# Softmax attention mixed with linear attention: the order of the attention rounds turned from head group first to query block first

## The chip, the cores and the metric

The kernel runs on one core of one Trainium2 chip. The metric is the device time of one execution in microseconds (us), as the median of several runs. One execution of the kernel before was also profiled; durations below come from that one.

## The reference

```
x = A_x                                          # 2048 x 512, bf16
g = sigmoid((x * gate_w).sum(-1))                # one gate per row
a = softmax(q k^T / 4) v  @ A_wo                 # q,k,v = x @ A_wqkv, 32 heads of 16
phi(t) = where(t > 0, t + 1, exp(t)) + 1e-6
kv = phi(k)^T v ; z = sum over rows of phi(k)    # q,k,v = x @ B_wqkv, 32 heads of 16
b = (phi(q) kv) / (phi(q) z + 1e-6)  @ B_wo
out = g * a + (1 - g) * b                        # 2048 x 512
```

The scores of branch A are 32 heads x 2048 x 2048 exponentials. Branch B has no exponential over pairs, only those of phi.

## The kernel before

**Rounds.** Branch A is cut into 32 rounds. A round r has one query block `qc` (512 queries, four of them), one head group `t8` (8 heads, four of them) and a parity `par` (four heads j of the eight). In a round, all 16 key blocks `kb` of 128 keys are taken with the four heads: 64 units of 128 keys x 512 queries. `rinfo(r)` says which round is which. Before, the head group is the outermost: rounds 0 to 7 are head group 0 with all four query blocks, rounds 8 to 15 head group 1, and so on:

```python
def rinfo(r):
    t8, k = divmod(r, 8)
    return k // 2, t8, k % 2
```

**Who takes the exponentials.** Most units go to ScalarE: `emit_act_group` issues the score matmuls (K^T against `QP`, 32 rows each, packed by rows of the array) for a group of three units (PSUM banks 0, 1, 2) or two (banks 3, 4), in turn, and one exp over the group into a `PT` slot (L915). The last key blocks of a round may go to VectorE: `d_claim` gives it a whole key block (four units) at a time, `d_s1` reads scores from banks 5 and 6, one or two banks at a time, into `Lb` (L1158), and `chain_op` makes the exponential from bit operations on 128 x 2048 elements in four instructions (L1181, L1184, L1187, L1190). The results `Xb`, `Eb`, `Lb` and `PT` are multiplied with `V` (`emit_pv`, `emit_dpv`), packed by columns, and summed in bank 7. At a round's end `round_end` transposes bank 7 into `U` (L1005); after every second round `t_norm` normalises, multiplies with the gate and transposes into `OT` (L1017 to L1024).

**The other work** consists of tasks that share banks 5 and 6 with VectorE's scores: `t_xtr` (transposes of x), `t_kproj`, `t_qproj`, `t_v0`, `t_v1` (projections of branch A; `t_v0` makes V of head group 0 and `t_v1` V of the other three), `t_gate`, and for branch B `t_phik`, `t_z`, `t_g`, `t_kv`, `t_phiq`, `t_den`, `t_num`, and `t_out` (both output projections and the store). `t_qproj` writes a projection to `QT`, from which eight DMAs on SP's queue bring it masked into `QP` (three slots). `t_num` writes numerators to `OB`, and four transposing DMAs on the same queue bring them to `OBT`.

**What sets the order.** The program is put in order while it is built. A planner keeps a clock for each engine with a cost for each operation, and picks the next one for PE among candidates: a score group for ScalarE, scores for VectorE, value matmuls, tasks. Each task has a due time and an earliest start, both in rounds (`add(key, generator, due, nb, pre)`), and `progress()` is the round that ScalarE's groups have reached. `need(key)` finishes a task on the spot when a candidate can't do without it. Where PE would stand idle, the planner puts in filler matmuls on a tile `warm`. The engines then run their lists in order, with semaphores; nothing is reordered on the chip. All matmuls but those of `t_xtr` have the line L373, the DMAs L306 and L310.

**Buffers.** `OT` (normalised output of branch A) has four slots, one for each query block; its third slot holds the first weights `wA0` at the start. `OBT` (branch B) has four slots too, which lie on other tiles: two on `phiK`, one on `wBv`, one on `GT`. `D0` and `DR0` say from which progress and for which round VectorE may take key blocks.

Of the kernel before, what the change touches and what calls it, by code (L numbers as in the profile page):

```python
# [10 lines left out]
BF16 = mybir.dt.bfloat16  # L11
# [134 lines left out]
def bass_gated_mix__mha_block__linear_attn_block__prompt_kernel(  # L146
# [14 lines left out]
    NTB = S // 128  # L161
# [11 lines left out]
    with ExitStack() as es:  # L173
# [20 lines left out]
        phiK = SB("phiK", [128, NTB, D], BF16)  # L194
        U = SB("U", [128, 2, 512], FP32)
        Tn = SB("Tn", [128, 16, 32], BF16)
        OT = SB("OT", [128, 4, 4, 512], BF16)
        ebuf = SB("ebuf", [128, 2, 512], BF16)
        GT = SB("GT", [128, NCC, D], BF16)
        KVbd = SB("KVbd", [128, 4, 128], BF16)  # L200
# [25 lines left out]
        OB = wA[:, 1, :, :]  # L226
        outt = wA[:, 2, :, :]
        phk = phiK[:].rearrange("p t c -> p (t c)")
        OBT = [phk[:, 0:2048].rearrange("p (i n) -> p i n", i=4), phk[:, 2048:4096].rearrange("p (i n) -> p i n", i=4), wBv[:], GT[:]]
        woA = phk[:, 4096:6144].rearrange("p (i n) -> p i n", i=4)  # L230
        woB = phk[:, 6144:8192].rearrange("p (i n) -> p i n", i=4)

# [30 lines left out]
        r_phiK = [R(f"phiK{i}") for i in range(NTB)]  # L263
        r_U = [R("U0"), R("U1")]
        r_Tn = R("Tn")
        r_OT = [[R(f"OT{s}_{a}") for a in range(4)] for s in range(4)]
        r_e = [R("e0"), R("e1")]
        r_GT = [R(f"GT{c}") for c in range(NCC)]
        r_KVbd = R("KVbd")
# [5 lines left out]
        r_OBT = [[R(f"OBT{s}_{b}") for b in range(4)] for s in range(4)]  # L275
        r_const = R("const")
        r_ident = R("ident")
        r_mask = R("mask")
# [366 lines left out]
        def t_num(qc, q):  # L645
            s = qc % 2
            sl = q % 4
            b = yield "bank"
            rd = r_phiQT[s] + [r_KVbd]
            yield ("pe", rd, [r_bk[b]], 1.4)  # L650
            pe([mm(BK[b][:, 128 * i:128 * (i + 1)], phiQT[:, s, i, 128 * q:128 * (q + 1)], KVbd[:, i, :]) for i in range(4)],
               reads=rd, writes=[r_bk[b]], waves=1.4, cols=512)
            yield ("dve", [r_bk[b], r_denB], [r_OB[sl]])
            op(DV, lambda: nc.vector.tensor_tensor(OB[:, sl, :].rearrange("p (h d) -> p h d", h=32), BK[b].rearrange("p (h d) -> p h d", h=32),
                                                   denB[:, q, :].unsqueeze(2).to_broadcast([128, 32, 16]), ALU.mult),
               reads=[r_bk[b], r_denB], writes=[r_OB[sl], r_wA[1]], cost=0.69)
            yield "free"
            alias = (r_phiK[0:8], r_phiK[0:8], [r_wBv], r_GT)[qc]
            for i in range(4):
                raw = dma(OBT[qc][:, i, 128 * q:128 * (q + 1)], OB[:, sl, 128 * i:128 * (i + 1)], f"obt{sl}",  # L660
                          reads=[r_OB[sl]], writes=[r_OBT[qc][q]] + alias if i == 0 else [], transpose=True, lat=2.5 + i)
            for x in [r_OBT[qc][q]] + alias:
                x.w = _Raw(dma_sems[f"obt{sl}"][0], dma_sems[f"obt{sl}"][1], raw.t)
                x.r = {}

        def t_out(qc, q):
            so = qc
            sl = (4 * qc + q) % 4
            qb = 4 * qc + q
            b = yield "bank"  # L670
            ops_ = [(OBT[qc][:, i, 128 * q:128 * (q + 1)], woB[:, i, :], [r_OBT[qc][q]]) for i in range(4)]
# [168 lines left out]

        def kq_aps(r, kb, j):
            qc, t8, par = rinfo(r)
            s = (4 * t8 + qc) % 3
# [155 lines left out]

        def round_end(r):  # L1000
            qc, t8, par = rinfo(r)
            so = qc
            if r > par + 1:
                need(("pair", r - par - 1))
            op(DV, lambda: nc.vector.transpose(U[:, par, :], acc), reads=[r_acc], writes=[r_U[par]], cost=0.71)  # L1005
# [4 lines left out]
                tasks.insert(0, t)  # L1010

        def t_norm(qc, t8):
            so = qc
# [219 lines left out]
        GN = .9  # L1233
        XT = [("xtr", t) for t in range(NQC)]
        for t in range(NQC):
            add(("xtr", t), t_xtr(t), 0.25 * t - 0.3)
# [2 lines left out]
                add(("Q", 0, 0), t_qproj(0, 0), -0.19, pre=[("xtr", 0)])  # L1239
            add(("V0", t), t_v0(t), 0.25 * t - 0.15, pre=[("xtr", t)])  # L1240
        for tb in range(NTB):
            k = 15 - tb if tb > 11 else 4 + tb
            add(("V1", tb), t_v1(tb), V1D + V1S * k, V1N + V1S * k, pre=XT)
        add(("gate",), t_gate(), GD, GN, pre=XT)
        for t8 in range(1, 4):
            for k, t in enumerate((3, 0, 1, 2)):
                due = 8 * t8 - 1.2 + 0.25 * k
                add(("K", t8, t), t_kproj(t8, t), due, KN * t8 + 0.4 * k, pre=XT)
        for n in range(1, 16):
            t8, qc = divmod(n, 4)  # L1250
            add(("Q", qc, t8), t_qproj(qc, t8), 2 * n - 0.9, 2 * n - 1.5, pre=XT)
        for tb in range(NTB):
            add(("phiK", tb), t_phik(tb), 100 + tb, PKN + PKS * tb, pre=XT)
        PK = [("phiK", tb) for tb in range(NTB)]
        PK1 = PKN + PKS * 16
        add(("wq",), t_wq(), 116, PK1, pre=PK)
        add(("z",), t_z(), 117, PK1, pre=PK)
        for k, cc in enumerate((2, 3, 0, 1)):
            add(("G", cc), t_g(cc), 118 + k, PK1 + 0.2 + 0.8 * k, pre=PK + ([("G", 3)] if cc < 2 else [("G", 2)] if cc == 3 else []))
        GA = [("G", c) for c in range(4)]  # L1260
        G1 = PK1 + 3.6
        add(("wo",), t_wo(), 123, G1, pre=GA + [("z",)])
        add(("kv",), t_kv(), 124, G1, pre=GA)
        for qc in range(NQC):
            b0 = G1 + 0.6 + BS * qc
            for i in range(4):
                add(("phiQ", qc, i), t_phiq(qc, i), 130 + 20 * qc + i, b0 + BS / 6 * i,
                    pre=[("wq",)] + GA + [("num", qc - 2, q) for q in range(4) if qc >= 2])
            add(("den", qc), t_den(qc), 135 + 20 * qc, b0 + BS * 2 / 3,
                pre=[("phiQ", qc, i) for i in range(4)] + [("z",), ("gate",)] + [("num", qc - 1, q) for q in range(4) if qc])  # L1270
            for q in range(4):
                add(("num", qc, q), t_num(qc, q), 136 + 20 * qc + q, b0 + BS * 2 / 3 + 0.1 + 0.2 * q,
                    pre=[("den", qc), ("kv",), ("K", 3, 3), ("K", 3, 0), ("K", 3, 1), ("K", 3, 2), ("z",)])
# [145 lines left out]
```

The softmax here doesn't subtract the row's maximum and nothing guards it: scores larger than these inputs give would overflow.

## Time and profile before

| | |
|---|---|
| median of 6 runs | 777.78 us (777.18 to 778.91) |
| the profiled execution | 777.3 us; span of its instructions 775.5 us |
| granted TensorE clock in it | 0.999 |
| PE busy | 734.6 us (95%), fillers included |
| VectorE (DVE) busy | 701.9 us (91%) |
| ScalarE (ACT) busy | 758.7 us (98%) |
| exps on ScalarE | 655 groups: 327 of 1536 columns, 327 of 1024, one of 512 |
| key blocks on VectorE | 103 of 512 |

Busy times of one engine are unions: instructions that overlap are counted once. In a row of the groups, the numbers behind the bar are busy time in us and the mean of one in ns, and then the idle time of the engine ahead of them with what ended it. In a row of the timeline, the first two numbers are start and length in us, and `x` counts instructions that were merged into one row.

### The profile page before, as it was taken

Reading aid. Unit: us, or ns where it says so; the run is one execution under the profiler, and the core shown is the slowest. Engines: PE = TensorE matmul, PEld = TensorE weight load, DVE = VectorE, ACT = ScalarE, POOL = GpSimd, SP = SyncE. Lnnn points to the kernel's source line nnn. Section 1 sums busy time; section 2 is a strip of 40 time slices with the busy share of each in tenths; the row PEclk is TensorE's granted clock in tenths of the full one; section 3 lists DMA queues with packets and bytes.
Section 4 is the critical chain, followed back from the end, with each engine's and each line's share of the span. In section 5 each row is a group of like instructions: output and inputs, shape, how many; then the busy total and the mean of one; then the engine's idle time right before and its main releaser. Section 6 shows DMA issues by size and latency. Waiting matters only on the chain.

```text
span 775.5 us, 18041 instructions
## 1 busy us (share of the span) xinstructions
PE 734.6 (95%) x7845; PEld 221.3 (29%) x7905; DVE 701.9 (91%) x978; ACT 758.7 (98%) x692; POOL 10.8 (1%) x36
## 2 busy tenths in 40 slices
PE   8999999999999999999999999999999999999997
PEld 3322232322222222222222233222232232222222
DVE  4399999999999999988988999999899998998996
ACT  5999999999999999999999999999999999999995
POOL 4000000000000000010000000000000000000000
PEclk9999999999999999999999999999999999999999
DMA  7200000000000000102010000101001000011000
GB/s 175 89 3 2 8 2 7 3 1 8 2 8 2 4 6 1 36 1 59 4 56 8 2 8 4 23 11 22 14 8 21 11 1 28 15 22 35 9 21 28
DMA packets 31342, 14.93 MB, mean 19 GB/s; under 512 B 19104, under 2 KB 31264, under 8 KB 31264
## 3 DMA queue, kind: packets, MB, share of 16 engines
q1 hardware_dynamic: 29392, 13.00, 6.5%
q8 instruction: 62, 1.02, 0.5%
q10 hardware_dynamic: 1872, 0.79, 0.4%
q14 instruction: 16, 0.13, 0.1%
HBM read 6.55 MB, written 2.10 MB: 11 GB/s over the span
## 4 chain that ended last, share of the span: by engine, by line
ACT 88%; PE 5%; DVE 4%; issue 2%; DMA 1%; DVEq 0%; SPq 0%; ACTq 0%
ACT sb_PT L915 85%; PE ps L373 5%; ACT sb_ebuf L554 2%; DVE sb_Lb L1158 2%; DMA sb_xT<-in_A_x_dram 1%; DVE sb_Xb L1187 0%; DVE sb_Xb L1181 0%; DVE sb_Eb L1184 0%; DVE sb_phiK L558 0%; DVE sb_rowt L535 0%; SPq L306 0%; DVE sb_Lb L1190 0%; DVE sb_KT L476 0%; DVE sb_U L1005 0%; ACT sb_wA L683 0%
## 5 line engine op out<-in xcount | busy, mean ns | idle before, releaser
L915 ACT ACTIVATE sb_PT<-ps 128x1536 bf16<-128x1536 f32 (+1 forms) x655 | 751.2, 1432 | 6.3 <-PE ps L373 6.2
L373 PE MATMUL ps<-sb_QP,sb_KT 32*128 32x512 bf16 x2048 | 307.1, 384 | 22.7 <-ACT sb_PT L915 12.5
L1158 DVE TENSOR_SCALAR sb_Lb<-ps 128x1024 uint16<-128x1024 f32 (+1 forms) x272 | 261.1, 961 | 36.6 <-PE ps L373 33.4
L373 PE MATMUL ps<-sb_warm 128*17 128x512 bf16 (+9 forms) x2200 | 200.9, 342 | 1.3 <-POOL sb_warm L411 1.3
L373 PEld LDWEIGHTS ps<-sb_QP,sb_KT 32*128 32x128 bf16 x2048 | 78.3, 91 | 288.7 <-ACT sb_PT L915 222.2
L373 PE MATMUL ps<-sb_PT,sb_V 128*17 128x512 bf16 x1636 | 154.5, 384 | 1.1 <-DVE sb_U L1005 0.9
L1187 DVE TENSOR_TENSOR sb_Xb<-sb_Xb,sb_Lb 128x2048 bf16<-128x2048 bf16 x103 | 125.3, 1216 | 0.0
L373 PEld LDWEIGHTS ps<-sb_warm 128*17 128x17 bf16 (+2 forms) x2201 | 61.8, 90 | 53.1 <-issue 28.3
L1181 DVE TENSOR_SCALAR sb_Xb<-sb_Lb 128x2048 uint16<-128x2048 uint16 x103 | 70.8, 687 | 1.2
L1184 DVE TENSOR_SCALAR sb_Eb<-sb_Lb 128x2048 uint16<-128x2048 uint16 x103 | 70.5, 684 | 0.0
L1190 DVE TENSOR_SCALAR sb_Lb<-sb_Lb 128x2048 uint16<-128x2048 uint16 x103 | 70.4, 684 | 0.0
L373 PEld LDWEIGHTS ps<-sb_PT,sb_V 128*17 128x17 bf16 x1636 | 36.9, 87 | 94.5 <-issue 87.8
L373 PE MATMUL ps<-sb_Xb,sb_V 128*17 128x512 bf16 x412 | 40.1, 380 | 0.5 <-DVE sb_Xb L1187 0.4
L373 PE MATMUL ps<-sb_Eb,sb_V 128*17 128x512 bf16 x412 | 40.2, 381 | 0.3 <-DVE sb_Eb L1184 0.2
L373 PE MATMUL ps<-sb_Lb,sb_V 128*17 128x512 bf16 x412 | 40.2, 380 | 0.0
L373 PE MATMUL ps<-sb_xT,sb_wA 128*128 128x512 bf16 x91 | 27.3, 382 | 3.7 <-issue 2.4
L554 ACT ACTIVATE sb_ebuf<-ps 128x512 bf16<-128x512 f32 x32 | 26.2, 817 | 0.0
L1005 DVE STREAM_TRANSPOSE sb_U<-ps 128x512 f32<-128x512 f32 x32 | 22.7, 709 | 2.7 <-PE ps L373 2.5
L373 PE MATMUL ps<-sb_wA,sb_xT 128*128 128x128 bf16 (+1 forms) x128 | 19.5, 275 | 0.3 <-DVE sb_phiK L558 0.3
L373 PE MATMUL ps<-sb_phiK,sb_OT 128*128 128x512 bf16 x63 | 18.2, 382 | 0.2 <-issue 0.2
L373 PE MATMUL ps<-sb_xT,sb_wBx 128*128 128x512 bf16 x54 | 16.4, 382 | 1.5 <-issue 1.1
L476 DVE CAST sb_KT<-ps 128x512 bf16<-128x512 f32 x16 | 11.0, 685 | 7.4 <-PE ps L373 7.4
(87 smaller groups left out, 299.3 us busy)
## 6 DMA issues: line engine op xcount, KB each, us to landing
sb_QP<-sb_QT SPq DMA_DIRECT2D x120, 16.0 KB, 1.8
out_dram<-sb_wA SPq DMA_DIRECT2D x14, 128.0 KB, 1.7
sb_wA<-in_A_wqkv_dram SPq DMA_DIRECT2D x2, 512.0 KB, 6.9
sb_wBx<-in_B_wqkv_dram SPq DMA_DIRECT2D x2, 512.0 KB, 6.2
sb_xnat<-in_A_x_dram SPq DMA_DIRECT2D x2, 512.0 KB, 4.0
sb_xnat<-in_A_x_dram SPq DMA_DIRECT2D x3, 256.0 KB, 3.2
sb_wBv<-in_B_wqkv_dram SPq DMA_DIRECT2D x1, 512.0 KB, 9.4
sb_phiK<-in_A_wo_dram SPq DMA_DIRECT2D x1, 512.0 KB, 3.6
```

The costliest lines, as they stand in the source:

```text
L373: return lambda: nc.tensor.matmul(o, lhsT=l, rhs=r, start=start, stop=stop, skip_group_check=sg)
L476: op(DV, lambda: nc.vector.tensor_copy(KT[:, t8, 512 * t:512 * (t + 1)], BK[b]), reads=[r_bk[b]], writes=[r_KT[t8][t]], cost=0.69)
L554: op(AC, lambda: nc.scalar.activation(ebuf[:, s, :], BK[b], ACT.Exp), reads=[r_bk[b]], writes=[r_e[s]], cost=0.48)
L915: op(AC, lambda: nc.scalar.activation(PT[:, slot, 0:512 * n], ps[:, 512 * set_[0]:512 * (set_[0] + n)], ACT.Exp, scale=SCALE), reads=wr, w ...
L1005: op(DV, lambda: nc.vector.transpose(U[:, par, :], acc), reads=[r_acc], writes=[r_U[par]], cost=0.71)
L1158: op(DV, lambda: nc.vector.tensor_scalar(Lb[:, sl, 512 * k:512 * (k + n)], src, S1A, S1B, op0=ALU.mult, op1=ALU.add), reads=[r_bk[b] for b ...
L1181: op(DV, lambda: nc.vector.tensor_scalar(X, L, 0x7F, 0x3F00, op0=ALU.bitwise_and, op1=ALU.bitwise_or), reads=[rl], writes=[rx], cost=CH[0])
L1184: ev = op(DV, lambda: nc.vector.tensor_scalar(E_, L, 0xFF80, None, op0=ALU.bitwise_and), reads=[rl], writes=[re_], cost=CH[1])
L1187: ev = op(DV, lambda: nc.vector.tensor_tensor(xb, xb, lb, ALU.mult), reads=[rx, rl], writes=[rx], cost=CH[2])
L1190: ev = op(DV, lambda: nc.vector.tensor_scalar(L, L, float(EXP_SH), None, op0=ALU.add), reads=[rl], writes=[rl], cost=CH[3])
```

## The change

The rounds are ordered by query block first: rounds 0 to 7 are query block 0 with all four head groups. Q projections, their slots and K slots follow. With this order the normalised outputs of a query block are complete after eight rounds, so `OT` has three slots in place of four (`so = qc % 3`), `OBT` has two, both on `phiK`, and `t_num` of block qc waits for the outputs of block qc - 2. The output tasks of a block become due after its eighth round (`8 * qc + 8.1`), where they were due at round 26 and later. All K projections are due before round 6 (due times 1.3 to 2.1, 3.1 and 5.1) and the V projections around round 1.5 to 2.2, with their earliest starts at 0.3 for V and head group 1 of K. `D0` goes from 1 to 0.8, `DR0` from 0 to 1, `RES` from 0.2 to 0.5. `t_gate` and `t_z` are as they were.

```diff
@@
-        OT = SB("OT", [128, 4, 4, 512], BF16)
+        OT = SB("OT", [128, 3, 4, 512], BF16)
...
-        OBT = [phk[:, 0:2048].rearrange("p (i n) -> p i n", i=4), phk[:, 2048:4096].rearrange("p (i n) -> p i n", i=4), wBv[:], GT[:]]
+        OBT = phk[:, 0:4096].rearrange("p (s i n) -> p s i n", s=2, i=4)
...
         def t_qproj(qc, t8):
-            n = 4 * t8 + qc
+            n = 4 * qc + t8
...
         def t_out(qc, q):
-            so = qc
+            s = qc % 2
+            so = qc % 3
...
-                        yield ("wait", ("pair", 25 + 2 * qc))
+                        yield ("wait", ("pair", 8 * qc + 7))
...
-        D0 = 1
-        DR0 = 0
+        D0 = .8
+        DR0 = 1
...
         def rinfo(r):
-            t8, k = divmod(r, 8)
-            return k // 2, t8, k % 2
+            qc, k = divmod(r, 8)
+            return qc, k // 2, k % 2
...
-        RES = .2
+        RES = .5
...
-        V1D = 3
-        V1N = 1.5
-        V1S = .25
+        V1D = 1.3
+        V1N = .3
+        V1S = .06
+        K1D = 1.3
         MH2 = .9
-        KN = 6
-        PKN = 2.5
-        PKS = 0.65
-        BS = 2.4
-        GD = 1.6
-        GN = .9
+        GD = 1.9
+        GN = .5
...
-            k = 15 - tb if tb > 11 else 4 + tb
-            add(("V1", tb), t_v1(tb), V1D + V1S * k, V1N + V1S * k, pre=XT)
+            add(("V1", tb), t_v1(tb), V1D + (0.05 * (15 - tb) if tb > 12 else V1S * (tb + 4)), V1N, pre=XT)
...
-            for k, t in enumerate((3, 0, 1, 2)):
-                due = 8 * t8 - 1.2 + 0.25 * k
-                add(("K", t8, t), t_kproj(t8, t), due, KN * t8 + 0.4 * k, pre=XT)
-        for n in range(1, 16):
-            t8, qc = divmod(n, 4)
-            add(("Q", qc, t8), t_qproj(qc, t8), 2 * n - 0.9, 2 * n - 1.5, pre=XT)
+            for t in range(4):
+                if t8 == 1:
+                    due = K1D + (0.3, 0.55, 0.8, 0)[t]
+                    add(("K", t8, t), t_kproj(t8, t), due, V1N, pre=XT)
+                    continue
+                add(("K", t8, t), t_kproj(t8, t), 2 * t8 - 0.9 + 0.1 * t, 2 * t8 - 1.8 + 0.2 * t,
+                    pre=XT)
+        for q4 in range(1, 16):
+            qc, t8 = divmod(q4, 4)
+            due = K1D + 0.25 if q4 == 1 else 2 * q4 - 0.9
+            add(("Q", qc, t8), t_qproj(qc, t8), due, due - 0.6, pre=XT)
...
-                    pre=[("den", qc), ("kv",), ("K", 3, 3), ("K", 3, 0), ("K", 3, 1), ("K", 3, 2), ("z",)])
+                    pre=[("den", qc), ("kv",), ("K", 3, 3), ("z",)] + ([("out", qc - 2, q)] if qc >= 2 else []))
...
-                add(("out", qc, q), t_out(qc, q), 140 + 20 * qc + q, 26.05 + 2 * qc + 0.35 * q if qc < 3 else 31.9,
-                    pre=[("num", qc, q), ("wo",)] + [("V1", tb) for tb in range(NTB)] + ([("pair", 25 + 2 * qc)] if qc < 3 else []))
+                add(("out", qc, q), t_out(qc, q), 140 + 20 * qc + q, max(17.2 + 3.0 * qc + 3.0, 8 * qc + 8.1) + 0.3 * q if qc < 3 else 31.9,
+                    pre=[("num", qc, q), ("wo",)] + ([("pair", 8 * qc + 7)] if qc < 3 else []))
```

The earliest starts of branch B's tasks are near those before; written as numbers, they are 2.5 + 0.65 per `t_phik`, and 17.2 + 3.0 per query block for `t_phiq`, `t_den` and `t_num`, where the latter had 2.4 per block from 17.1.

More of the change, by code (lines that the diff above doesn't have):

```diff
@@ L265, in bass_gated_mix__mha_block__linear_attn_block__prompt_kernel @@
         r_Tn = R("Tn")
-        r_OT = [[R(f"OT{s}_{a}") for a in range(4)] for s in range(4)]
+        r_OT = [[R(f"OT{s}_{a}") for a in range(4)] for s in range(3)]
         r_e = [R("e0"), R("e1")]
@@ L274, in bass_gated_mix__mha_block__linear_attn_block__prompt_kernel @@
         r_outt = [R(f"outt{i}") for i in range(4)]
-        r_OBT = [[R(f"OBT{s}_{b}") for b in range(4)] for s in range(4)]
+        r_OBT = [[R(f"OBT{s}_{b}") for b in range(4)] for s in range(2)]
         r_const = R("const")
@@ L657, in t_num @@
             yield "free"
-            alias = (r_phiK[0:8], r_phiK[0:8], [r_wBv], r_GT)[qc]
             for i in range(4):
[L660 to L664, printed above, removed]
+                raw = dma(OBT[:, s, i, 128 * q:128 * (q + 1)], OB[:, sl, 128 * i:128 * (i + 1)], f"obt{sl}",
+                          reads=[r_OB[sl]], writes=[r_OBT[s][q]] + r_phiK[0:8] if i == 0 else [], transpose=True, lat=2.5 + i)
+            r_OBT[s][q].w = _Raw(dma_sems[f"obt{sl}"][0], dma_sems[f"obt{sl}"][1], raw.t)
+            r_OBT[s][q].r = {}
+            for x in r_phiK[0:8]:
+                x.w = r_OBT[s][q].w
         def t_out(qc, q):
-            so = qc
+            s = qc % 2
+            so = qc % 3
             sl = (4 * qc + q) % 4
@@ L670, in t_out @@
             b = yield "bank"
-            ops_ = [(OBT[qc][:, i, 128 * q:128 * (q + 1)], woB[:, i, :], [r_OBT[qc][q]]) for i in range(4)]
+            ops_ = [(OBT[:, s, i, 128 * q:128 * (q + 1)], woB[:, i, :], [r_OBT[s][q]]) for i in range(4)]
             ops_ += [(OT[:, so, a, 128 * q:128 * (q + 1)], woA[:, a, :], [r_OT[so][a]]) for a in range(4)]
@@ L842, in kq_aps @@
             qc, t8, par = rinfo(r)
-            s = (4 * t8 + qc) % 3
+            s = (4 * qc + t8) % 3
             return (KT[32 * j:32 * j + 32, t8, 128 * kb:128 * (kb + 1)], QP[32 * j:32 * j + 32, s, par, :],
@@ L1001, in round_end @@
             qc, t8, par = rinfo(r)
-            so = qc
+            so = qc % 3
             if r > par + 1:
@@ L1012, in t_norm @@
         def t_norm(qc, t8):
-            so = qc
+            so = qc % 3
             yield ("wait", ("gate",))
@@ L1252, in bass_gated_mix__mha_block__linear_attn_block__prompt_kernel @@
         for tb in range(NTB):
-            add(("phiK", tb), t_phik(tb), 100 + tb, PKN + PKS * tb, pre=XT)
+            add(("phiK", tb), t_phik(tb), 100 + tb, 2.5 + 0.65 * tb, pre=XT)
         PK = [("phiK", tb) for tb in range(NTB)]
-        PK1 = PKN + PKS * 16
-        add(("wq",), t_wq(), 116, PK1, pre=PK)
-        add(("z",), t_z(), 117, PK1, pre=PK)
+        add(("wq",), t_wq(), 116, 13, pre=PK)
+        add(("z",), t_z(), 117, 13, pre=PK)
         for k, cc in enumerate((2, 3, 0, 1)):
-            add(("G", cc), t_g(cc), 118 + k, PK1 + 0.2 + 0.8 * k, pre=PK + ([("G", 3)] if cc < 2 else [("G", 2)] if cc == 3 else []))
+            add(("G", cc), t_g(cc), 118 + k, 13.2 + 0.8 * k, pre=PK + ([("G", 3)] if cc < 2 else [("G", 2)] if cc == 3 else []))
@@ L1260, in bass_gated_mix__mha_block__linear_attn_block__prompt_kernel @@
         GA = [("G", c) for c in range(4)]
-        G1 = PK1 + 3.6
-        add(("wo",), t_wo(), 123, G1, pre=GA + [("z",)])
-        add(("kv",), t_kv(), 124, G1, pre=GA)
+        add(("wo",), t_wo(), 123, 16.6, pre=GA + [("z",)])
+        add(("kv",), t_kv(), 124, 16.6, pre=GA)
         for qc in range(NQC):
-            b0 = G1 + 0.6 + BS * qc
             for i in range(4):
-                add(("phiQ", qc, i), t_phiq(qc, i), 130 + 20 * qc + i, b0 + BS / 6 * i,
+                add(("phiQ", qc, i), t_phiq(qc, i), 130 + 20 * qc + i, 17.2 + 3.0 * qc + 0.5 * i,
@@ L1268, in bass_gated_mix__mha_block__linear_attn_block__prompt_kernel @@
                     pre=[("wq",)] + GA + [("num", qc - 2, q) for q in range(4) if qc >= 2])
-            add(("den", qc), t_den(qc), 135 + 20 * qc, b0 + BS * 2 / 3,
+            add(("den", qc), t_den(qc), 135 + 20 * qc, 17.2 + 3.0 * qc + 2.0,
                 pre=[("phiQ", qc, i) for i in range(4)] + [("z",), ("gate",)] + [("num", qc - 1, q) for q in range(4) if qc])
             for q in range(4):
-                add(("num", qc, q), t_num(qc, q), 136 + 20 * qc + q, b0 + BS * 2 / 3 + 0.1 + 0.2 * q,
-                    pre=[("den", qc), ("kv",), ("K", 3, 3), ("K", 3, 0), ("K", 3, 1), ("K", 3, 2), ("z",)])
+                add(("num", qc, q), t_num(qc, q), 136 + 20 * qc + q, 17.2 + 3.0 * qc + 2.1 + 0.2 * q,
+                    pre=[("den", qc), ("kv",), ("K", 3, 3), ("z",)] + ([("out", qc - 2, q)] if qc >= 2 else []))
```

## The prediction

> **What bounds the kernel now.** I read the page's busy times, slices and chain first, then the groups of instructions by shape, then two stretches of the timeline.
>
> ```profile
> span 775.5 us, 18041 instructions
> ...
> PE 734.6 (95%) x7845; PEld 221.3 (29%) x7905; DVE 701.9 (91%) x978; ACT 758.7 (98%) x692; POOL 10.8 (1%) x36
> ...
> DVE  4399999999999999988988999999899998998996
> ACT  5999999999999999999999999999999999999995
> ...
> ACT 88%; PE 5%; DVE 4%; issue 2%; DMA 1%; DVEq 0%; SPq 0%; ACTq 0%
> ```
>
> ScalarE is full from its first exp to its last and carries 88% of the chain. PE's 95% holds filler matmuls on `warm`; VectorE has idle time almost only in its first two slices (0 to 39 us).
>
> ```profile
> L915 ACT ACTIVATE sb_PT<-ps 128x1536 bf16<-128x1536 f32 x327 | 537.3, 1643 | 6.3 <-PE ps L373 6.2
> L915 ACT ACTIVATE sb_PT<-ps 128x1024 bf16<-128x1024 f32 x327 | 400.2, 1224 | 0.0
> L1158 DVE TENSOR_SCALAR sb_Lb<-ps 128x1024 uint16<-128x1024 f32 x140 | 170.7, 1219 | 13.9 <-PE ps L373 12.7
> L1187 DVE TENSOR_TENSOR sb_Xb<-sb_Xb,sb_Lb 128x2048 bf16<-128x2048 bf16 x103 | 125.3, 1216 | 0.0
> L1158 DVE TENSOR_SCALAR sb_Lb<-ps 128x512 uint16<-128x512 f32 x132 | 90.4, 687 | 22.6 <-PE ps L373 20.7
> ```
>
> The exps overlap: 537.3 + 400.2 is more than ScalarE's whole busy time. So an idle time of 6.3 us doesn't tell how long exps were late; their start times do.
>
> ```profile
> 89.58 0.80 ACT L554 ACTIVATE sb_ebuf<-ps 128x512 bf16<-128x512 f32 x1
> 90.05 2.58 ACT L915 ACTIVATE sb_PT<-ps 128x1536 bf16<-128x1536 f32 x2
> 92.29 0.84 ACT L554 ACTIVATE sb_ebuf<-ps 128x512 bf16<-128x512 f32 x1
> 92.77 24.30 ACT L915 ACTIVATE sb_PT<-ps 128x1536 bf16<-128x1536 f32 x21
> 116.79 0.77 ACT L554 ACTIVATE sb_ebuf<-ps 128x512 bf16<-128x512 f32 x1
> ```
>
> A pair of groups (1536 and 1024 columns) takes 92.29 - 90.05 = 2.24 us, a 512 one 0.48; start by start, the least distances are 1.331 and 0.904. The 21 groups from 92.77 then need 11 x 1.331 + 10 x 0.904 = 23.68, and took 24.02: 0.34 us of lateness that idle time doesn't show. Over the whole run: exps go from 9.77 to 766.17, 756.4 us. Their work is 327 x 1.331 + 327 x 0.904 + 33 x 0.478 + 0.16 (the gate's) = 746.8, and the last one's tail 0.28. So **9.3 us are hidden lateness**, spread evenly. The rest is head (9.8) and tail (775.5 - 766.17 = 9.3).
>
> ```profile
> 744.68 0.39 PE L373 MATMUL ps<-sb_QP,sb_KT 32*128 32x512 bf16 x4
> 745.01 0.60 PE L373 MATMUL ps<-sb_phiK,sb_OT 128*128 128x512 bf16 x2
> 745.55 0.39 PE L373 MATMUL ps<-sb_QP,sb_KT 32*128 32x512 bf16 x2
> 745.87 0.61 PE L373 MATMUL ps<-sb_PT,sb_V 128*17 128x512 bf16 x8
> 746.41 0.60 PE L373 MATMUL ps<-sb_phiK,sb_wBv 128*128 128x512 bf16 x2
> 746.95 0.39 PE L373 MATMUL ps<-sb_QP,sb_KT 32*128 32x512 bf16 x4
> ```
>
> From these starts I price PE: one step of 512 columns (a full matmul, up to four row-packed score matmuls, or four column-packed value matmuls) 0.215, and 0.10 more where the shape changes (0.33 for a score step, 0.54 for two full ones). A feed (the score matmuls of one exp group) may start when the group two before it has left its banks. With ends of 1.643 and 1.224 after their starts, 0.06 to the next matmul and its 0.39, PE can put about **1.46 us of work between two feeds** before the next exp is late; 0.48 more where an `ebuf` exp lies there.
>
> **The change part by part.** *What its name says.* Gate logits and sums of phi(K) are in both kernels the same 16 + 16 matmuls of 512 columns and five 32x32 transposes. Cost of that: nothing. What the diff does is to turn the rounds from head group first to query block first.
>
> *Exps moved off ScalarE.* In the changed kernel's instruction order VectorE takes 104 key blocks instead of 103. ScalarE loses one 1536 and one 512 group: -1.331 - 0.478 = **-1.81 us**, on the path.
>
> *VectorE pays for it:* one chain more (0.687 + 0.684 + 1.216 + 0.684 = 3.27) and 127 double plus 162 single reads of PSUM in place of 140 and 132: 30 x 0.687 - 13 x 1.219 = 4.76. Together +8.0 us on 701.9. Its 73.6 us of idle time covers it, so 0 here; uncovered it would be the whole 8.0.
>
> *Projections moved forward.* Counts are equal, places aren't. All 16 `t_v1` copies (549 ns) fall in rounds 0 to 2 (4, 6, 6 by the transposes that end rounds) instead of 1 to 5; the K projections of head groups 1, 2, 3 lie in rounds 0 to 5 instead of 6-7, 12-13, 18-19. Priced as above, PE's work without fillers in rounds 1 to 3 rises from 55.7 to 66.1 us, of about 69.5 us of ScalarE time; fillers fall from 10.2 to 2.9. That is where the cover shrinks. Interval by interval, work over 1.46 between feeds: before, 19 intervals, 1.75 us in all; after, 31 intervals, 3.89. The worst stands in round 2: one projection `K(1,2)`, put directly before the scores that read it because they need it at once, then a V projection forced in the same way (`V1(7)`), give 2.55 us of work between two feeds, 1.1 too much. Everything queued on PE behind waits, the next feed first, and ScalarE for that. So the direct count adds 3.89 - 1.75 = +2.1. But the 9.3 us measured are 5.3 times what is counted, for a late feed also follows from PE waiting for VectorE to empty a bank; in the same ratio the change would add 2.14 x 5.3 = +11.4. I take **+4.0**, nearer the direct count: the other waits were spread over the run and not tied to full intervals.
>
> [...]
>
> *The end of the run.* In the changed order two output stores follow the last QP transfers on SP; before, nine. What this saves in full intervals of rounds 26 to 31 is in the count. After the last exp the chain is the same (values, transpose, normalisation, transpose, output matmuls, copies, store), but four output matmuls follow the last transpose rather than nine. The four copies run one after the other either way (770.53 to 773.23), and can start one or two matmuls earlier: -0.2, between -0.4 and +1 if VectorE's last chain comes later than the last exp (it idled 1.36 us there).
>
> *Buffers and queues.* Three OT and two OBT slots make the numerators of block qc wait for the outputs of qc - 2; the order has these whole rounds earlier: 0. SP still issues 120 QP transfers and 64 transposes. QP parts now stand behind stores and transposes, but are planned 0.9 rounds (21 us) before their reader and land in 1.8: 0; if one were late, up to 1.8 us each.
>
> Sum: -1.81 - 0.2 + 4.0 = +2.0. The profiled execution took 777.3 (1.8 outside the span), so it becomes 779.3; the median of the runs is 0.5 above it at 777.78, so **779.8**.
>
> **The rivals.** *The crowd is absorbed (faster).* Lateness stays at 9.3 us: rounds 1 to 3 still hold less PE work than exp time, and overfull intervals may fall where ScalarE is behind anyhow. Then -2.0 remains: 775.8. It decides if added lateness stays under 0.4 us. Against it speaks the 2.55 us interval alone.
>
> *Lateness scales (much slower).* Between the transposes that end rounds 1 and 2 VectorE has 45 instructions of 27.6 us by their rows; each next one starts some 0.08 before the former ends, which leaves 24.0, beside 52 units of exp at 0.447 (a pair's 2.235 over five), 23.2. If banks 5 and 6 then stay held and feeds queue behind, +11.4 - 2.0 gives 787.2.
>
> *It doesn't do what it says, and the turn is neutral.* Gain and loss cancel with 2 us of added lateness: 777.8.
>
> **How the numbers follow.** A measurement of this kernel tells 0.2%, 1.56 us (776.2 to 779.3), from no change. The forecast's bounds are -2.0 + 2.1 = +0.1 and +9.4. Absorbed: 0.15, faster. Neutral: 0.12, same. Lateness in the full ratio: 0.05, slower. The forecast 0.68: 0.20 of it with under 3.6 us of added lateness, hence within 0.2%, and 0.48 above. That makes 0.15, 0.32 and 0.53. The range from 776.0 to 786.0 leaves out most of the absorbed case and the full ratio.
>
> **What would show it.** Right: 653 exp groups, a distance sum of 745.0, hidden lateness near 13 us with most of the growth before 100 us, and a gap of about 1 us around the K(1,2) projection near 75 us. Wrong: exps as even in rounds 1 to 3 as before (then 775.8), or lateness grown evenly through all rounds, which would point to VectorE and not to the crowd. A chain with VectorE above 10% would also contradict me.

## The result, and the profile after

The changed kernel takes **780.02 us** (median of 19 runs, 778.24 to 783.38) against 777.37 for the kernel before (median of 43 runs, 776.93 to 779.1): a ratio of 1.0032, 95% interval 1.0023 to 1.0040. The profiled execution took 780.02 with a span of 778.2, so 1.8 us lie outside the span as before. In eight of the 14 profiles here, whichever kernel, the first exp starts near 11.4 us instead of 9.7 (run 2 below shows why); spans of single profiles are therefore compared by their parts. The ratio and its interval are those on record; here and below, a ratio need not be the quotient of the two medians.

The page of the changed kernel (lines of the source stand one higher than before: the exps are L916, VectorE's reads of scores L1159):

```profile
span 778.2 us, 17861 instructions
...
PE 730.8 (94%) x7750; PEld 220.1 (28%) x7817; DVE 706.7 (91%) x999; ACT 757.9 (97%) x690; POOL 10.3 (1%) x36
...
DVE  4499899899999998999899999989999999999995
...
ACT 83%; PE 8%; DVE 6%; issue 2%; DMA 1%; DVEq 0%; SPq 0%; ACTq 0%
```

And the groups of instructions, shapes kept apart:

```profile
L916 ACT ACTIVATE sb_PT<-ps 128x1536 bf16<-128x1536 f32 x326 | 529.1, 1623 | 9.2 <-PE ps L373 9.1
L916 ACT ACTIVATE sb_PT<-ps 128x1024 bf16<-128x1024 f32 x327 | 393.1, 1203 | 0.3 <-PE ps L373 0.3
...
L1159 DVE TENSOR_SCALAR sb_Lb<-ps 128x1024 uint16<-128x1024 f32 x127 | 154.7, 1218 | 10.2 <-PE ps L373 9.0
L1188 DVE TENSOR_TENSOR sb_Xb<-sb_Xb,sb_Lb 128x2048 bf16<-128x2048 bf16 x104 | 126.5, 1217 | 0.0
L1159 DVE TENSOR_SCALAR sb_Lb<-ps 128x512 uint16<-128x512 f32 x162 | 110.7, 686 | 23.7 <-PE ps L373 22.5
```

One group of 1536 columns less, the single 512 one gone, 104 key blocks on VectorE. ScalarE's share of the chain fell from 88% to 83%, PE's rose from 5% to 8%. Exps go from 9.86 to 769.25. By the prediction's distances their work is 326 x 1.331 + 327 x 0.904 + 32 x 0.478 + 0.16 = 744.97, the last one's tail 0.19, so 14.2 us are lateness, where before it was 9.33:

| us | before | after | difference |
|---|---|---|---|
| work of the exps | 746.78 | 744.97 | -1.81 |
| lateness, start to 100 us | 1.61 | 3.89 | +2.28 |
| lateness, 300 to 325 and 450 to 475 us | 0.23 | 3.62 | +3.39 |
| lateness elsewhere | 7.49 | 6.72 | -0.77 |
| head, the last exp's own tail, and what follows it | 19.37 | 19.02 | -0.35 |
| span | 775.5 | 778.2 | +2.7 |

The lateness of each stretch is the sum of the distances between exp starts, less the least distance of each shape. Two stretches have grown, and the second is one that the prediction had not named. This is the first, in the timeline (start, length, then what ran):

```profile
75.75 0.39 PE L373 MATMUL ps<-sb_QP,sb_KT 32*128 32x512 bf16 x3
...
76.07 1.04 PE L373 MATMUL ps<-sb_xT,sb_wA 128*128 128x512 bf16 x4
76.15 0.71 DVE L535 STREAM_TRANSPOSE sb_rowt<-ps 128x512 f32<-128x512 f32 x1
76.89 0.17 DVE L536 COPY sb_gl<-sb_rowt 128x16 f32<-128x16 f32 x1
...
77.10 0.26 ACT L539 ACTIVATE sb_eg<-sb_gl 128x64 f32<-128x64 f32 x1 [0.66 <-DVE sb_gl L536]
...
77.26 1.43 ACT L916 ACTIVATE sb_PT<-ps 128x1536 bf16<-128x1536 f32 x1
...
77.53 0.82 PE L373 MATMUL ps<-sb_wA,sb_xT 128*128 128x384 bf16 x4
...
78.61 0.60 PE L373 MATMUL ps<-sb_QP,sb_KT 32*128 32x512 bf16 x5
...
79.04 1.02 ACT L916 ACTIVATE sb_PT<-ps 128x1024 bf16<-128x1024 f32 x1 [0.35 <-PE ps L373]
```

The four matmuls at 76.07 are `K(1,2)`, those at 77.53 `V1(7)`, as predicted; the scores at 78.61 come behind them and the exp at 79.04 is 0.45 us late. But the larger wait, 0.77 us, is ahead of that. The exp of the gate (L539) stands in ScalarE's list and waits for VectorE's last transpose of the gate logits (L535, L536), and the score exp at 77.26 is queued behind it, though its scores were there.

The second stretch shows in a table of windows (start and end, length, then the busy time and number of instructions of PE, weight load, VectorE, ScalarE and GpSimd; the first number behind these is the granted TensorE clock):

```profile
299.70:303.10 3.40, 2.44 (x24) 0.64 (x20) 3.01 (x5) 3.40 (x5) 0.00 (x0) 1.00 0.00 0
303.10:306.50 3.40, 3.40 (x29) 0.70 (x33) 2.58 (x5) 2.84 (x3) 0.00 (x0) 0.50 0.02 5
463.60:467.00 3.40, 2.34 (x24) 0.71 (x27) 3.07 (x5) 3.40 (x5) 0.00 (x0) 0.99 0.08 19
467.00:470.40 3.40, 3.40 (x33) 0.66 (x25) 2.57 (x4) 2.56 (x3) 0.00 (x0) 0.50 0.00 0
```

From 303.1 and from 467.0 us, PE runs at **half its clock**; in the trace's record of the clock both stretches last 3.413 us. The stretch ahead of each is thin: 24 matmuls, 2.44 and 2.34 us busy of 3.40. Both are ends of rounds: VectorE transposes bank 7 in them (at 301.59 and 465.43 us), and the planner put only single filler matmuls there. Over the rest of the run fillers are not fewer than before: behind round 3 the records have 1820 column fillers on `warm`, against 1748. It is their places that have changed. At half clock a score step takes 0.56 to 0.60 us instead of 0.39, the next feeds come late, and ScalarE idles (2.84 and 2.56 us busy of 3.40). The mean clock is 0.997 to 0.998 in the seven shortest runs that have a clock on record (778.24 to 778.65), 0.995 in the profiled one, and 0.991 to 0.992 in the three longest (782.49 to 783.38). A half-clock window takes 0.0022 of the mean (half of 3.413 us in 778), and the half clock at the very end takes 0.0004 in the profiled run and up to 0.0017 in others (run 5). By that estimate the runs have one, two or three windows. In the 80 runs of the kernel before beside the experiments the mean clock was 0.999 to 1.0, but for four at 0.997.

### The profile page after: what moved, and what is told of

Read it like the earlier page. It is cut to its first block, busy times and chain, and to the rows that moved or that the text cites. A ratio compares the mean times of both kernels' runs of the same rounds, so it can differ in the third digit from the quotient of the medians.

```text
span 778.2 us, 17861 instructions
## 1 busy us (share of the span) xinstructions
PE 730.8 (94%) x7750; PEld 220.1 (28%) x7817; DVE 706.7 (91%) x999; ACT 757.9 (97%) x690; POOL 10.3 (1%) x36
## 4 chain that ended last, share of the span: by engine, by line
ACT 83%; PE 8%; DVE 6%; issue 2%; DMA 1%; DVEq 0%; SPq 0%; ACTq 0%
ACT sb_PT L916 81%; PE ps L373 8%; ACT sb_ebuf L554 2%; DVE sb_Lb L1159 2%; DVE sb_Xb L1188 1%; DMA sb_xT<-in_A_x_dram 1%; DVE sb_Xb L1182 0%; DVE sb_Eb L1185 0%; DVE sb_U L1006 0%; DVE sb_rowt L535 0%; DVE sb_Lb L1191 0%; DVE sb_V L525 0%; DVE sb_Tn L1021 0%; DVE sb_xnat L558 0%; DVE sb_OT L1025 0%
## 5 line engine op out<-in xcount | busy, mean ns | idle before, releaser
L916 ACT ACTIVATE sb_PT<-ps 128x1536 bf16<-128x1536 f32 (+1 forms) x653 | 749.4, 1413 | 9.6 <-PE ps L373 9.4
L1159 DVE TENSOR_SCALAR sb_Lb<-ps 128x512 uint16<-128x512 f32 (+1 forms) x289 | 265.4, 920 | 33.9 <-PE ps L373 31.5
L373 PE MATMUL ps<-sb_warm 128*17 128x512 bf16 (+8 forms) x2101 | 192.9, 341 | 1.5 <-POOL sb_warm L411 1.3
L373 PEld LDWEIGHTS ps<-sb_warm 128*17 128x17 bf16 (+2 forms) x2105 | 59.8, 91 | 49.4 <-issue 27.2
L373 PE MATMUL ps<-sb_phiK 128*128 128x512 bf16 x54 | 16.6, 382 | 1.7 <-issue 1.1
```

The lines of the kernel that those rows point to most:

```text
L373: return lambda: nc.tensor.matmul(o, lhsT=l, rhs=r, start=start, stop=stop, skip_group_check=sg)
L916: op(AC, lambda: nc.scalar.activation(PT[:, slot, 0:512 * n], ps[:, 512 * set_[0]:512 * (set_[0] + n)], ACT.Exp, scale=SCALE), reads=wr, w ...
L1159: op(DV, lambda: nc.vector.tensor_scalar(Lb[:, sl, 512 * k:512 * (k + n)], src, S1A, S1B, op0=ALU.mult, op1=ALU.add), reads=[r_bk[b] for b ...
```

## Experiments

Two explanations are weighed. The crowd: the projections that were moved into rounds 0 to 2 make PE and VectorE late. The clock: thin stretches of PE's work bring half-clock windows, which make the feeds late.

**1. The thin places filled.** The changed kernel with nine filler steps put into PE's finished list, eight of them as below and one near 303 us behind a transpose of bank 7: the planner and every other engine's order are untouched.

```diff
+        zf = [mm(acc[32 * j:32 * j + VW, :], warm[:, 0:VW], warm, start=False, stop=False, sg=True) for j in range(4)]
+        more = [(pvat[k], n, []) for k, n in {153: 2, 242: 3, 281: 3}.items()]
...
+            PE.ops[at:at] = [(w if k == 0 else [], f, False, None) for k, f in enumerate(zf * n)]
```

> The changed kernel, order and semaphores untouched, with nine more column-packed filler steps of 512 columns on the zero tile, put where PE stands idle in the trace of after: two near 300.2 us, one near 302.5, three near 464.2, three near 537.5. Clock theory (the two stretches of 3.41 us at half clock in the profile of after, from 303.1 and 467.0 us, cost by themselves some 1.7 us each, and come because too few columns stream in the 3.41 us before): no half-clock stretch is left in most runs, the lateness of the exps falls from 14.1 to about 10.7 us, the median falls by 2.5 to 3.5 us to 776.5 to 777.5. Crowd theory (late exps around 303 and 468 us come from PE work and VectorE waits in the order, the low clock only follows from an idle PE): the order is the same, so time stays within 1 us of 780.0, or grows by up to 2 us for the added steps.

Measured: 778.81 us (12 runs), ratio 1.0015, interval 1.0004 to 1.0026. Both windows are gone and lateness in their slices fell from 3.62 to 0.87 us, but one stands at 513.0 us now, and its slice has 1.84 us (0.57 in run 9, where it is gone). So the clock is a cause, and nine steps don't fill every thin place: the mean clocks are 0.995 to 0.997 in all runs but one. The time and the lateness that the clock theory expected (776.5 to 777.5, and 10.7 us; the profile has 13.1) were therefore missed.

**2. The kernel before, filled.** Two filler steps of the same kind near 510 us, its thinnest place.

> The kernel before, order and semaphores untouched, with two more filler steps near 510.4 and 511.4 us. Clock theory: its runs fall into two heaps, about 777.2 and 778.9, because one place (508 to 512 us) is thin enough to lower the clock in about half of the runs; with the steps the upper heap goes, nearly all runs are 777.0 to 777.5, and the median moves by 0 to -0.3. Crowd theory: the two heaps stay as they are.

Measured: 777.23 us, ratio 0.9998, interval 0.9988 to 1.0007. Nothing to gain there: the kernel before hardly has half-clock windows. The two heaps stay, eight runs at 776.9 to 777.4 and four at 778.9 to 779.0, so the thin place doesn't make them. The profiled run (779.01) is one of the upper heap, and its first exp starts at 11.50 us instead of 9.77. The eight matmuls of the first projections, ahead of that exp, tell why. First the profile of the kernel before, then this run's:

```profile
6.60 1.89 PE L373 MATMUL ps<-sb_xT,sb_OT 128*128 128x512 bf16 x8 [0.83 <-DMA sb_xT<-in_A_x_dram]
```

```profile
6.49 3.57 PE L373 MATMUL ps<-sb_xT,sb_OT 128*128 128x512 bf16 x8 [0.71 <-DVE sb_xT L464]
```

From start to start one takes 0.427 us here and 0.215 there: PE still runs at half clock. The trace's record of the clock begins with the first full clock, at 10.77 us here and at 6.46 there, and the mean of 1.0 leaves out what lies ahead of it. All 14 profiles divide that way: with full clock by 6.46 us the first exp is at 9.64 to 9.99 (six), with full clock from 10.06 us or later at 11.34 to 11.55 (eight). So the 1.7 us between the heaps are a matter of the clock after all, at the start of the run.

**3. The gate earlier.** `GD` from 1.9 to 1.2 in the changed kernel, so that its exp isn't queued in the crowd near 75 us.

> The changed kernel with the gate's due time at 1.2 rounds in place of 1.9, so that its four matmul groups, transposes and its exp are over before the K(1,2) and V projections of round 2 (the planner then orders all of the run anew; 104 key blocks on VectorE as before). Crowd theory: lateness between 60 and 95 us falls from about 2.4 us to under 1, and the time falls by as much or more. Clock theory says the same of these 35 us (0.8 us there was the gate's exp waiting for VectorE), and that the rest of the run depends on how many thin places the new order has: 1.7 us more or less for each.

Measured: 779.45 us, ratio 1.0024, interval 1.0014 to 1.0034. Lateness before 100 us is 4.12 instead of 3.89: it has only moved to 70 us, where a K projection waits for the copy of a V projection (L525) that stands behind a normalisation on VectorE, and the feed behind both is 1.56 us late. Two windows of half clock (539.5 and 730.7 us) are there too. So moving the gate's exp alone doesn't cure the crowd; as all of the order changed with it, the run doesn't price it.

**4. Fillers made thin in the kernel before.** The converse of the first: the same kernel and order, but the planner's column fillers stream 64 columns instead of up to 512.

```diff
-pe([mm(acc[32 * j:32 * j + VW, 0:w], warm[:, 0:VW], warm[:, 0:w], start=False, ...) for j in range(4)],
+pe([mm(acc[32 * j:32 * j + VW, 0:64], warm[:, 0:VW], warm[:, 0:64], start=False, ...) for j in range(4)],
```

> The kernel before with the same order, but each of its column-packed filler steps streams 64 columns in place of 128 to 512: less PE work, nothing else changed. Clock theory: counted from the trace of before without these columns, some 15 windows of 3.41 us fall under 0.47 of streaming; each lowers the clock for one window and costs 1 to 1.7 us, so +12 to +25 us (789 to 802), and the granted clock falls to about 0.96. Crowd theory: PE has less to do and the exps bound the time, so 777.4 or up to 2 us less, at any clock.

Measured: 798.49 us, ratio 1.0271, interval 1.0251 to 1.0291. Less work for PE, and 21 us more. From the page, and from a table of windows around 577 us:

```profile
PEclk9977999999999999999989999999969999999899
```

```profile
574.00:577.20 3.20, 2.36 (x40) 0.87 (x37) 2.69 (x6) 3.20 (x5) 0.00 (x0) 1.00 0.02 5
577.20:590.80 13.60, 13.47 (x134) 4.18 (x126) 10.63 (x14) 10.88 (x10) 0.00 (x0) 0.50 0.00 1
```

The clock record has 21 windows of 3.413 us at half clock (four in a row from 577.2), and lateness rose from 9.33 to 28.91 us: 0.93 per window. The mean clock is 0.954 in this profile, where it is 0.999 in that of the kernel before. This settles that matmuls which compute nothing held the clock here, and gives a mean price of a window.

**5. All thin places filled, with waits.** 32 filler steps in the changed kernel instead of nine (26 in the expectation).

> The changed kernel with its order untouched and 26 filler steps of 512 columns (9 from the run before, 17 more) in the thin places that are left: near 164, 231 to 234, 279 to 281, 511 to 513, 538, 727 to 729, 745 and 748 us. If half-clock windows are what the first 100 us don't explain, none are left: granted clock 0.999, lateness of 100 to 750 us as in the kernel before, span 775.4 to 775.8 with the early head, time 777.2 to 777.6. So the change would be level with the kernel before: -1.81 (ScalarE's units) and -0.35 (tail) against +2.3 (lateness before 100 us). Rival: the turned order has lateness of its own in the later rounds, which fillers don't cure: 778.5 to 780 at a clock of 0.999, or the fillers delay the feeds and cost more.

Measured: 793.94 us, ratio 1.0199, interval 1.0184 to 1.0215. The rival's second half came true. The timeline tells why:

```profile
165.12 0.39 PE L373 MATMUL ps<-sb_PT,sb_V 128*17 128x512 bf16 x4
166.39 0.70 DVE L1011 STREAM_TRANSPOSE sb_U<-ps 128x512 f32<-128x512 f32 x1
167.15 0.53 PE L373 MATMUL ps<-sb_warm 128*17 128x512 bf16 x4 [1.64 <-DVE sb_U L1011]
167.60 0.61 PE L373 MATMUL ps<-sb_QP,sb_KT 32*128 32x512 bf16 x3
...
168.26 2.37 ACT L918 ACTIVATE sb_PT<-ps 128x1536 bf16<-128x1536 f32 x2 [1.54 <-PE ps L373]
```

These fillers write bank 7, so at a round's end they wait for its transpose, here for 1.64 us, in a list that is run in order; the feed behind them waits as well, and the clock of PE, now truly idle, falls to half on top (four windows, mean clock 0.990).

**6. The 104th key block by itself.** The kernel of the fifth run with `d_claim` stopped at 103 key blocks; only the last round's order differs.

```diff
-            if r >= NR or progress() < D0:
+            if r >= NR or progress() < D0 or sum(claimed) >= 103:
```

> The kernel with 26 filler steps, with VectorE's key blocks stopped at 103 instead of 104: order equal up to the last round, where four units go back to ScalarE. Prices the prediction's unit term by itself. If the 1.81 us lie on the path: +1.8 against the run beside it (779.0 to 779.4). Rival: the 104th key block is worth less, since the last round ends with VectorE's chains and values, which come earlier without it: +0.5 or less.

Measured: 793.24 us; the two kernels' windows of half clock vary too much for the medians to tell. Their two profiles, with the same four windows and the same head, have spans of 791.2 and 793.2. The last run below does it cleanly.

**7. The crowd alone, without the turn.** The kernel before with the V and K projections moved forward as in the change.

```diff
-            k = 15 - tb if tb > 11 else 4 + tb
-            add(("V1", tb), t_v1(tb), V1D + V1S * k, V1N + V1S * k, pre=XT)
+            add(("V1", tb), t_v1(tb), 1.3 + (0.05 * (15 - tb) if tb > 12 else .06 * (tb + 4)), .3, pre=XT)
...
+                if t8 == 1:
+                    due, nb = 1.3 + (0.3, 0.55, 0.8, 0)[t], .3
+                else:
+                    due, nb = 2 * t8 - 0.9 + 0.1 * t, 2 * t8 - 1.8 + 0.2 * t
```

> The kernel before with its rounds not turned, but with the V projections of t_v1 due and allowed as in the changed kernel (due 1.3 to 2.2, start 0.3), and the K projections of head group 1 too (1.3 to 2.1), those of groups 2 and 3 in rounds 2 to 5: the crowd alone, 103 key blocks. If the crowd costs what its overfull intervals say: lateness before 100 us +1.5 to +2.5, and as it leaves rounds without work for PE later, one or two half-clock windows of 1.0 to 1.7 us: 779.5 to 782. Rival: the turn itself (slots, masks, order of Q transfers) makes the lateness, and the crowd is absorbed: 777.3.

Measured: 782.73 us, ratio 1.0054, interval 1.0039 to 1.0069; the profile has no half-clock window, though one or two were expected. Lateness before 100 us is 2.74, 1.13 more than before and less than the expected 1.5 to 2.5; the gate's exp is in it here too, 0.86 us late. Then one single feed at 334.4 us is 2.27 late: eleven matmuls of a `t_g` task lie ahead of it. The crowd costs something without the turn, but the planner also answers with another order later on, so this run doesn't price it alone.

**8. Not turned, four constants changed.** The kernel before with one key block more on VectorE, found by letting the planner build orders with other constants.

```diff
-        RES = .2
+        RES = .5
...
-        KN = 6
-        PKN = 2.5
+        KN = 5.5
+        PKN = 3
...
-        BS = 2.4
+        BS = 2.6
```

> The kernel before, not turned, with four constants of the planner changed (RES 0.2 to 0.5 as in the change, KN 6 to 5.5, PKN 2.5 to 3, BS 2.4 to 2.6). VectorE takes 104 key blocks in the order that results, and no projection is forced. If a key block more is worth 1.81 and only the crowd and the half-clock windows take it back in the changed kernel: 775.0 to 775.8, clock 0.998 or more. Rival: the 104th key block fills VectorE (91% busy already), so that scores wait for banks and the lateness rises by as much: 777 or more.

Measured: 775.55 us, ratio 0.9979, interval 0.9966 to 0.9991. 104 key blocks, lateness before 100 us 1.41, and -1.7 us: the work term of the prediction, with no crowd and, by the mean clocks (0.999 to 1.0), in six of ten runs no half-clock window to take it back. Its profile has one, at 724.1 us.

**9. The thin places filled, with nothing that waits.** The nine steps of the first run, and in 14 other places a feed's score matmuls issued twice, behind the wait that PE has there anyway.

```diff
+        for k in [389, 393, 397, 586, 590, 716, 720, 1354, 1357, 1361, 1937, 1941, 1991, 1998]:
+            at, n = qkn[k]                # where the score matmuls of a feed begin in PE's list, and how many
+            PE.ops[at:at] = [(w2, f, False, None) for w2, f, _, _ in PE.ops[at:at + n]]
```

> The changed kernel, order untouched, with the 9 filler steps of the first filler run (e1) and, in 14 places of the remaining thin stretches (162 to 164, 232 to 234, 279, 511 to 513, 726 to 728, 745, 748 us), a feed's score matmuls issued twice: the same result into the same banks, right behind the wait that PE has there anyway, so that 0.215 us more stream and nothing new waits. The filler run with 26 steps failed since the fillers themselves waited in PE's list. If half-clock windows are what the first 100 us don't explain: no or hardly a half-clock window, granted clock 0.998 to 0.999, span 775.5 to 776 with the early head, median 777.3 to 778. Rival: the later rounds have lateness of their own at full clock: 778.8 or more, as with 9 steps, at a clock of 0.999.

Measured: **777.65 us** (11 runs, 777.43 to 779.26), ratio 1.0009, interval 1.0000 to 1.0017, clocks of 0.998 to 1.0, and in the profile no window before the end. The windows that were half speed in the changed kernel:

```profile
299.70:303.10 3.40, 2.94 (x35) 0.83 (x32) 2.98 (x5) 3.40 (x5) 0.00 (x0) 1.00 0.00 0
303.10:306.50 3.40, 3.40 (x51) 1.05 (x51) 3.23 (x6) 3.40 (x4) 0.00 (x0) 1.00 0.00 0
463.60:467.00 3.40, 2.99 (x38) 0.93 (x38) 3.37 (x5) 3.40 (x4) 0.00 (x0) 1.00 0.02 5
467.00:470.40 3.40, 3.36 (x55) 1.15 (x47) 3.40 (x4) 3.40 (x5) 0.00 (x0) 1.00 0.02 5
```

35 and 38 matmuls in the stretch ahead instead of 24, and the clock stays at 1.00. As an estimate from the records, with 0.215 us for 512 columns (from start to start, run 2) and what runs side by side counted once, PE streams in some 60% of these two stretches, where it was some 45%; ahead of the window at 513 us in run 1 it was about 50%. Lateness is 11.95 us in place of 14.2; the first 100 us keep their 3.9, and all that comes after has 8.05, against 7.72 in the kernel before.

**10. Half of the moved projections' matmuls.** Run 9 with the first and third of the four matmuls of `t_v1` and `K(1,t)` taken out of PE's list.

> The same kernel, with two of the four matmuls left out of each of the 16 t_v1 projections and the four K projections of head group 1 (half of the contraction is missing from V of head groups 1 to 3 and K of group 1); copies, waits and order stay. That takes 32 x 0.16 + 8 x 0.215 = 6.8 us off PE before 95 us. If PE's overfull intervals make the lateness of the first 100 us (3.4 us in the changed kernel, 1.1 before): it falls to 1.5 to 2.2, what is left being the gate's exp that stands behind VectorE (0.8), and the time falls by 1.2 to 1.9 against the run beside it. Rival: it is VectorE, whose transposes and copies come late whatever PE does: 3.2 or more stays, same time.

Measured: 776.94 us, 0.7 below run 9, with 2.63 us of lateness from 25 to 100 us where run 9 has 3.40. Three of its eleven runs lie above 780 at clocks of 0.990 to 0.993: probably less work for PE thins other stretches, but none of the three has a profile. From the timeline:

```profile
76.87 0.26 ACT L539 ACTIVATE sb_eg<-sb_gl 128x64 f32<-128x64 f32 x1 [0.66 <-DVE sb_gl L536]
...
77.03 4.60 ACT L919 ACTIVATE sb_PT<-ps 128x1536 bf16<-128x1536 f32 x4
...
79.82 0.69 DVE L1027 TENSOR_TENSOR sb_Tn<-sb_U,sb_rden 128x512 bf16<-128x512 f32 x1
80.43 0.55 DVE L525 CAST sb_V<-ps 128x384 bf16<-128x384 f32 x1
...
81.04 0.39 PE L373 MATMUL ps<-sb_PT,sb_V 128*17 128x512 bf16 x4 [0.67 <-DVE sb_V L525]
```

The gap of 0.45 us behind `K(1,2)` and `V1(7)` is gone: four exps run from 77.03 on without a wait. The gate's exp waits as in the changed kernel, and the values at 81.04 wait for the copy of `V1(7)`, which VectorE does after a normalisation (L1027). That lies between the two theories: 0.8 of the 2.28 us goes with these matmuls, 1.5 stays. Two of the waits that stay are for VectorE's list by name: the gate's exp (0.77 us late) and the exp at 82.07 (0.57 us), whose feed stands behind those values. They make 1.34 of the 2.63 us; the remainder stays open.

**11. The best of both.** Run 8 with doubled score matmuls in seven thin places, the same edit as in run 9.

> The kernel that was not turned, with four planner constants changed (e6), and in seven places of its thinnest stretches (205 to 206, 441, 579, 721 to 724 us) a feed's score matmuls issued twice. Four of e6's ten runs held a clock of 0.996 to 0.997. If these were half-clock windows at its thin places: granted clock 0.999 in all runs, median 775.3 to 775.5, hardly a run between 776.2 and 776.9, and the ratio to the kernel before 0.9975 to 0.998, all of it below 1. Rival: the doubled matmuls delay feeds or VectorE's scores: 776 or more at a clock of 0.999.

Measured: **775.41 us** (12 runs, 775.11 to 777.01), ratio 0.9976, interval 0.9968 to 0.9985. Its profile has a clock of 0.999 and 9.20 us of lateness, where the kernel before has 9.33. This kernel beats both, with 104 key blocks and the rounds not turned. One run (776.64, at 0.997) is in the band that should have been nearly empty, against one of ten in run 8.

**12. The key block priced cleanly.** Run 9 stopped at 103 key blocks.

> The changed kernel without half-clock windows (e9: 777.65), with VectorE's key blocks stopped at 103 instead of 104, so that only the last round differs. If ScalarE's 1.81 us lie on the path: 779.4 to 779.7, work sum 746.78, lateness as in e9 (11.8). Rival: the last round's key block hides its cost behind VectorE's last chains: 777.6 to 778.2.

Measured: 779.65 us, ratio 1.0031, interval 1.0019 to 1.0043: 2.0 above run 9. By parts: work 746.78 against 744.97 (+1.81), lateness 11.91 against 11.95, tail 9.16 against 8.96.

## Why the prediction was right, and where its sum was not

By medians, the way from one kernel to the other is 777.3 (before), **+2.35** to 779.65 (turned, 103 key blocks, clock held), **-2.0** to 777.65 (the 104th key block), **+2.4** to 780.02 (half-clock windows).

*Exps moved off ScalarE, -1.81:* right, and on the path: run 12 shows it with only the last round's order changed, and runs 8 and 11 agree in an order that is not turned.

*VectorE, 0:* right, though its idle time was misread: only 24.6 of its 73.6 us lay in the first 39 us, the rest is spread over the run. Its busy time rose by 4.8 us, not by 8.0, and once the clock is held, the lateness after 100 us leaves little room for it (8.05 us in run 9, 7.72 before).

*Projections moved forward, +4.0:* the size is near the measured +4.9, but the step was composed wrongly. The direct count, 19 to 31 full intervals and +2.1 us, is close to the +2.28 of the first 100 us. I then raised it to 4.0 for waits of PE on VectorE. What came on top instead was the clock: 1.44 and 1.37 us in the two slices that run 9 cures (1.82 to 0.38, 1.80 to 0.43), with -0.2 elsewhere. The prediction saw fillers fall from 10.2 to 2.9 us in rounds 1 to 3 and priced only the lost cover there. It had no term for what fillers do in the 28 rounds after that: hold the clock through round ends (mean clock 0.995 in the changed kernel's profile, 1.0 in that of run 9). So its sign that "most of the growth" comes before 100 us failed, with 2.28 of 4.9. And the count's +2.1 fits better than its mechanism: of the 2.28, only 0.8 goes when half of the moved matmuls is taken out (run 10), and the largest single wait is that of the gate's exp (0.77 us), for which the prediction has no term. Of the gap of about 1 us that it expected around `K(1,2)`, 0.45 stands behind the projections. That 779.8 and the measured 780.02 are so near is in part luck: 1.9 us were added for one reason, and 2.6 came from another.

*The end of the run, -0.2:* measured -0.35. *Buffers and queues, 0:* nothing in the trace speaks against it; it was not tried by itself.

*The rivals.* "The crowd is absorbed" falls with the 2.28 us. "Lateness scales" (+11.4) too: lateness outside the first 100 us and the two windows' slices fell by 0.77. "Neutral" holds for the order without its half-clock windows: 777.65 against 777.3, where -1.81 and +2.28 cancel almost as that rival put it. Its own words, 2 us of added lateness, do not hold for the changed kernel, which has 4.9. What it lacks against the kernel of run 9 is cheap matmuls in eighteen places.

## What to carry to other kernels

When a new order moves fillers or leaves longer stretches in which nothing may be issued, price the clock as a term of its own: look for stretches of about 3.4 us in which PE streams about half the time or less (by the estimate of run 9, some 45% and about 50% ahead of half-clock windows here, some 60% where the clock stayed at 1.00), and count some 1 us for each (0.93 on average in run 4, 1.4 in the changed kernel). Not each of them lowers the clock: one at some 45% in run 9 kept it (from 700.6 us). A busy share of 94%, or a page whose clock digits are all 9 as in the changed kernel's, doesn't show them; a table of windows does. Nor does a mean clock of 1.0 show a slow start (run 2): the time of the matmuls ahead of the first exp does. And fill such a place with something that waits for nothing new, such as a matmul repeated behind a wait that is there already: a filler with a wait of its own stands ahead of the work in PE's list and can cost more than the clock (run 5: 14 us).

## What the runs showed of the hardware

The half-clock windows in the changed kernel's profile came after stretches without any long pause. The longest idle times of PE in the two stretches are 0.44 and 0.53 us ahead of 303.1, and 0.69 and 0.37 us ahead of 467.0. Each window then lasted 3.413 us; in run 4 up to four follow each other (13.65 us from 577.2, of which the table above has 13.60 at a clock of 0.50). Their number differs from run to run of one kernel: one to three in the changed one, by the mean clocks (0.998 to 0.991).

The record of the clock also shows how far apart its changes lie. In each of the 14 profiles all changes to half clock and back lie whole steps of 3.413 us apart: in the changed kernel the window at 303.13 begins 87 steps and that at 466.97 135 steps after the first full clock at 6.17. The place of these steps in the span differs from profile to profile: the first full clock comes anywhere from 4.03 to 6.46 or from 10.06 to 10.77 us. That this is why the same kernel gets one window or three is my estimate, which no run tests.

The streaming share alone doesn't tell where the clock falls. Run 9 streams some 45% in the 3.4 us from 700.6 us, which is one of its steps (204 after the first full clock at 4.28), and kept its clock, while the changed kernel lost it after two stretches of some 45%. What decides such a case stays open.
